# An index row between two gathers, and when the warm-up matmuls run

## The chip, the core and the metric

The kernel runs on one core of a Trainium2 chip. The time is the device time of one launch in microseconds (us); a run's time is taken without a profile, and one further execution is taken with the hardware profiler. TensorE (PE) multiplies, VectorE (DVE) and ScalarE (ACT) do elementwise work, GpSimd (POOL) makes indices and constants and issues the indirect DMAs, SyncE (SP) issues the other DMAs. Two DMA queues matter here: q1, which SP feeds, and q0, which POOL feeds. Both are served by the same 16 DMA engines.

## The reference

```python
x: (8, 3008, 256) float32
X = np.fft.fft(x, axis=1); X = np.fft.fft(X, axis=2); a = X.real      # both transforms, real part
h = np.maximum(a.reshape(24064, 256) @ w_in, 0.0)                     # w_in (256, 2048)
out = (h * h) @ w_out                                                 # w_out (2048, 256)
```

## The kernel before

The transform over the 256 features is linear, so it is multiplied into the first weight matrix: `gmat(c)` makes, for each of four blocks of 512 columns of `w_in`, the products of `w_in` with a cosine matrix (`pc`, kept as G1) and a sine matrix (`ps`, kept as G2). `gcast(c)` turns the float32 block `wst[c]` to float16 first: blocks 0 and 1 on ScalarE, 2 and 3 on VectorE. `dmats()` makes the cosine and sine matrix `csD` itself: from a row of descending numbers, `jrow`, that POOL writes (L149), four VectorE operations (L212 to L216), a fifth one later (L202), and two sines on ScalarE (L222, L223). `jrow` and its work space lie in `wst[0]`, that is, in the buffer into which the first quarter of `w_in` is loaded afterwards; so `load_w_in` (L760, four DMAs on SP) waits until L223 has read it.

The transform over the sequence uses its symmetry. A batch of 3008 rows is loaded twice: two plain loads by SP (slots 0 and 1 of `x4`) and the same rows in reversed order by indirect gathers on POOL (slots 2 and 3). For batch 0 the reversed rows come in four half gathers, `gather_half(0, s, q)` (L99), in the order slot 3 second half, slot 2 second half, slot 3 first half, slot 2 first half. VectorE adds the plain and the reversed rows (L360, L364, the "fold"), once for each half, then sums and differences (L369, L373) give `w`, the operand of the first matmuls. `stage1_first` runs these: nine matmuls on the first half (`s1[0]`), and three and six on the second half (`s1[1]`, `s1[2]`), against the tables `cosT` and `sinT`, into sums named `pf`. ScalarE copies one of each pair of sums (`as`, L484) and VectorE writes `pt` and `qt` (L493, L489).

From `pt`, `qt` and G each step (chunk c, part u) makes `xb` by TensorE, ScalarE and VectorE apply the ReLU and the square (`h`), and TensorE multiplies by `wout` into `po`, stored by SP. The first 16 `po` matmuls of a tile read the four quarters of `wout` in turn; these are loaded by four DMAs on POOL (`load_w_out`, L766), which stand behind the two gathers of batch 1 (`load_x(1)`, L112), which wait until the fold of batch 0 has read `x4` (L364).

The kernel's schedule is manual: each engine runs its instructions in the order in which the code issues them, with waits where data or buffers require them. Before the first sums, TensorE runs `warm_up(6)`: matmuls on a zeroed tile `ez`, whose result nothing reads; two more (`warm_up(2)`) stand between `s1[0]` and `gmat(0)`. They wait for POOL's memset of `ez` (L339), which stands behind the gathers and three index rows.

In the order of the code: the gathers and `jrow` (L145 to L151), tables and folds with the loads between them (L771 to L791), warm-ups and first sums (L798 to L812), and then the loop over the steps. L74 is the helper through which all matmuls go.

Of the kernel before, what the change touches and what calls it, by code (L numbers as in the profile page):

```python
# [24 lines left out]
def kernel(  # L25
# [7 lines left out]
    nc = tc.nc  # L33
    B, S, D = x.shape
    _, F = moe_w_in.shape
    P = 128
# [3 lines left out]
    QH = NQ // 2  # L40
# [32 lines left out]
    def mm(o, l, r, start, stop):  # L73
        nc.tensor.matmul(o, l, r, start=start, stop=stop, skip_group_check=True)  # L74

    def iota(name, shape, pattern, base, mult, dt=F32):
        t = const.tile(shape, dt, name=name)
        nc.gpsimd.iota(t, pattern=pattern, base=base, channel_multiplier=mult,
                       allow_small_or_imprecise_dtypes=True)
        return t  # L80
# [8 lines left out]
                   allow_small_or_imprecise_dtypes=True)  # L89
# [8 lines left out]
    def gather_half(b, s, q):  # L98
        nc.gpsimd.indirect_dma_start(  # L99
            out=x4[0:NP, 2 + s, q : q + QH, :].rearrange("p q d -> p (q d)"),  # L100
            out_offset=None,
            in_=bass.AP(tensor=x.tensor, offset=x.offset,
                        ap=[[QH * D, B * S // QH], [1, QH * D]]),
            in_offset=bass.IndirectOffsetOnAxis(ap=idx3[0:NP, 0:1], axis=0),
            element_offset=(b * S + (s + 1) * M - NQ * NP + q) * D)
# [16 lines left out]
    def load_mid(b, eng):  # L122
        for s in range(2):
            row = x[b : b + 1, s * M : s * M + 1]
            if b == 0:
                for sl, n in (((0, 1), (3, 1)), ((1, 2),))[s]:
                    eng.dma_start(out=x4[NP : NP + 1, sl : sl + n].rearrange("p s q d -> p (s q) d"),
                                  in_=row.to_broadcast([1, n * NQ, D]))
            else:
                r = s * NQ + 1  # L130
                r2 = (3 - s) * NQ + NQ - 2
                eng.dma_start(out=xm[:, r : r2 + 1 : r2 - r], in_=row.to_broadcast([1, 2, D]))
# [9 lines left out]
    for s in range(2):  # L142
        nc.sync.dma_start(out=x4[0:NP, s, :, :], in_=up(0, s))
    load_mid(0, nc.sync)
    for q in (QH, 0):  # L145
        for s in range(2):
            gather_half(0, 1 - s, q)
    jrow = jm[:, 0]
    nc.gpsimd.iota(jrow, pattern=[[-1, P]], base=P - 1, channel_multiplier=0,  # L149
                   allow_small_or_imprecise_dtypes=True)  # L150
    idx = iota("idx", [P, 1], [[0, 1]], NP - 1, -1, I32)  # L151
    idx2 = iota("idx2", [P, 1], [[0, 1]], NQ // 2 * (NP - 1), -NQ // 2, I32)
    wout16 = const.tile([P, NFC, D], F16, name="wout16")
# [161 lines left out]
    def win16(c):  # L315
        if c // 2 not in winh:
            winh[c // 2] = bfp.tile([P, 2, 1024], F16, name="win16", tag="w")
        return winh[c // 2][:, :, c % 2 * 512 : c % 2 * 512 + 512]

    def gcast(c, cp):  # L320
        cp(win16(c), wst[c])

    def gmat(c):
        cs = slice(c * 512, (c + 1) * 512)
        pc = psx.tile([P, 512], F32, name="pc", tag="x")
        for t in range(2):
            mm(pc, cosD[:, t, :], win16(c)[:, t, :], t == 0, t == 1)
        ps = psx.tile([P, 512], F32, name="ps", tag="x")
        for t in range(2):
            mm(ps, sinD[:, t, :], win16(c)[:, t, :], t == 0, t == 1)  # L330
        act(G1[:, cs], pc, AF.Copy, bias=0.0, scale=-1.0 / HS)  # L331
        act(G2[:, cs], ps, AF.Copy, bias=0.0, scale=1.0 / HS)  # L332

    def gneg(c):
        cs = slice(c * 512, (c + 1) * 512)
        ts(out=G3[:, cs], in0=G2[:, cs], scalar1=s3[:, 0:1], scalar2=None, op0=ALU.mult)
# [197 lines left out]
    for n in sizes:  # L534
        segs = []
        o = 0
        while o < n:
            b, i = divmod(g + o, NK)
# [255 lines left out]
    def warm_up(n):  # L794
        for _ in range(n):
            mm(warm, ez[:, 1, 0, :], ez[:, 1, 0:4, :], True, True)

    warm_up(6)  # L798
    gcast(0, nc.scalar.copy)
    hi_ops = []  # L800
    s1 = stage1_first(hi_ops)
    s1[0]()
    warm_up(2)
    gmat(0)
    s1[1]()
    s1[2]()
# [11 lines left out]
    side = {}  # L818
# [4 lines left out]
            side.setdefault(lo + int((hi - lo) * i / len(ops)), []).append(f)  # L823

    for c in range(1, F // 512):
        side.setdefault(c * (c - 1) // 2, []).extend([lambda c=c: gmat(c), lambda c=c: gneg(c)])

    spread(rd1[0:], 0, 5)
    spread(fo, 9, 10)
# [136 lines left out]
```

## Time and profile before

| | us |
|---|---|
| median of 4 runs (603.56 to 605.47) | 605.1 |
| the profiled execution, its own time | 602.61 |
| its span, first to last instruction | 600.7 |
| TensorE busy before 10 us / 10 to 23 / 23 to 46 / after 46 | 0.48 / 9.21 / 20.74 / 550.13 |
| VectorE busy in the same stretches | 6.41 / 8.98 / 22.67 / 485.95 |
| ScalarE busy | 7.41 / 7.84 / 22.25 / 510.81 |
| POOL busy | 8.12 / 5.25 / 0.88 / 149.97 |
| mean busy share of the DMA engines | 0.76 / 1.00 / 0.89 / 0.38 |
| memory traffic of the DMA, GB/s | 220 / 302 / 143 / 84 |

In a line of the timeline the first number is the start, the second the time from the first to the last end of a group of like instructions, then the engine, the line of the code, the operation, output and inputs, and in brackets the engine's idle time just before and what ended it. In a line of a DMA queue there stand packets, megabytes and the time of the packets as a share of 16 engines' time in the stretch.

### The profile page before, as it was taken

What the parts mean: (1) busy time and instruction counts of PE and PEld (TensorE: products, weight loads), DVE (VectorE), ACT (ScalarE), POOL (GpSimd) and SP (SyncE); (2) the same over time, 40 slices, a digit from 0 to 9 for tenths busy, and PEclk for the clock granted to TensorE, in tenths of its full rate; (3) what the DMA queues carried; (4) which work ended last, traced back from release to release, by engine and by line L of the source; (5) the groups of instructions that cost most, each with busy time, mean ns of one, the idle gap of its engine ahead of it and who ended that gap; (6) DMA issues with size and microseconds to landing.
All of it is one profiled execution on the core that took longest, in us unless ns stands there. A gap on an engine that the chain in (4) does not pass through costs nothing.

```text
span 600.7 us, 12237 instructions
## 1 busy us (share of the span) xinstructions
PE 580.6 (97%) x4543; PEld 436.4 (73%) x4543; DVE 524.0 (87%) x959; ACT 548.3 (91%) x963; POOL 164.2 (27%) x156
## 2 busy tenths in 40 slices
PE   1889999999999999999999999999999999999997
PEld 0566677777777777777877778777787778877786
DVE  6899898998898998897899997899889899999880
ACT  7799899999989999989998989999998999999981
POOL 5301023122331223213022143422543423324400
PEclk9999999999999999999999999999999999999999
DMA  8986485564583314813233115133242231332112
GB/s 225 303 98 165 103 244 174 166 224 56 69 239 45 60 55 87 222 40 49 54 59 45 53 39 68 36 47 57 57 63 42 54 49 55 51 55 56 56 53 71
DMA packets 41952, 56.24 MB, mean 94 GB/s; under 512 B 7746, under 2 KB 36726, under 8 KB 41894
## 3 DMA queue, kind: packets, MB, share of 16 engines
q1 hardware_dynamic: 37030, 42.04, 33.0%
q0 software_dynamic: 4864, 13.44, 8.8%
q8 instruction: 35, 0.57, 0.4%
q14 instruction: 23, 0.19, 0.1%
HBM read 29.02 MB, written 24.64 MB: 89 GB/s over the span
## 4 chain that ended last, share of the span: by engine, by line
PE 91%; ACT 5%; DMA 2%; DVE 1%; issue 1%; POOL 0%; ACTq 0%; DVEq 0%; POOLq 0%
PE po L74 53%; PE xb L74 31%; PE pf L74 6%; DMA x<-in_x_dram,idx 2%; ACT h L671 1%; ACT h L738 1%; ACT h L747 0%; ACT G L332 0%; ACT h L748 0%; ACT os L618 0%; ACT h L726 0%; POOL x L99 0%; ACT bs L713 0%; ACT G L331 0%; DVE bs L716 0%
## 5 line engine op out<-in xcount | busy, mean ns | idle before, releaser
L74 PE MATMUL po<-wout,h 128*128 128x256 f16 x3024 | 450.0, 272 | 0.7 <-ACT os L618 0.5
L74 PEld LDWEIGHTS <-h 128*128 128x128 f16 x3024 | 286.1, 98 | 110.4 <-issue 2.1
L74 PE MATMUL xb<-qt,G 128*128 128x512 f16 (+10 forms) x743 | 207.1, 321 | 1.6 <-ACT h L671 1.2
L714 POOL TENSOR_TENSOR bs<-bs,h 128x512 f32<-128x512 f32 x92 | 118.5, 1291 | 316.1 <-ACT bs L713 256.8
L727 DVE CUSTOM_DVE_ANT_0 h<-xb,bs 128x512 f16<-128x512 f32 (+1 forms) x231 | 145.0, 640 | 22.8 <-ACT h L726 20.6
L74 PE MATMUL xb<-pt,G 128*128 128x512 f16 (+16 forms) x512 | 146.3, 323 | 1.0 <-DVE h L727 0.4
L726 ACT ACTIVATE h<-xb 128x512 f16<-128x512 f32 (+1 forms) x218 | 135.4, 623 | 7.8 <-PE xb L74 5.5
L750 DVE TENSOR_TENSOR h<-h 128x2048 f16<-128x2048 f16 (+1 forms) x113 | 137.3, 1216 | 0.8 <-ACT h L738 0.7
L74 PEld LDWEIGHTS <-G 128*128 128x128 f16 x1255 | 120.2, 98 | 24.4 <-issue 3.4
L671 ACT ACTIVATE h<-xb 128x512 f16<-128x512 f32 (+1 forms) x166 | 104.1, 630 | 8.5 <-PE xb L74 7.6
L738 ACT ACTIVATE h<-xb 128x512 f16<-128x512 f32 (+2 forms) x155 | 96.0, 623 | 9.4 <-PE xb L74 7.8
L716 DVE SCALAR_TENSOR_TENSOR bs<-xb,h 128x512 f32<-128x512 f32 (+1 forms) x126 | 83.1, 660 | 18.7 <-PE xb L74 15.4
L748 ACT ACTIVATE h<-h 128x1024 f16<-128x1024 f16 (+1 forms) x79 | 84.8, 1074 | 0.0
L747 ACT ACTIVATE h<-h 128x1024 f16<-128x1024 f16 (+1 forms) x79 | 83.8, 1061 | 0.1
L697 DVE TENSOR_SCALAR h<-eb,gE 128x512 f16<-128x512 f16 (+1 forms) x198 | 70.3, 370 | 0.0
L618 ACT ACTIVATE os<-po 128x512 f32<-128x512 f32 (+1 forms) x95 | 59.5, 627 | 8.9 <-PE po L74 8.9
L713 ACT ACTIVATE bs<-xb 128x512 f32<-128x512 f32 x92 | 57.3, 623 | 3.2 <-PE xb L74 2.0
L112 POOL DMA_INDIRECT x<-in_x_dram,idx x16 | 21.0, 1313 | 77.0 <-DVE u L364 60.2
L360 DVE TENSOR_TENSOR u<-x 127x765 f16<-127x765 f32 x32 | 29.6, 950 | 1.3 <-DMA x<-in_x_dram,idx 1.3
L74 PEld LDWEIGHTS <-w 127*128 127x128 f16 (+1 forms) x192 | 22.2, 120 | 10.8 <-DVE w L373 4.5
L74 PE MATMUL pf<-cosT,w 127*128 127x377 f16 (+1 forms) x96 | 20.8, 329 | 3.9 <-DVE w L373 3.6
L373 DVE TENSOR_TENSOR w<-v 127x384 f16<-127x384 f16 x64 | 22.2, 371 | 0.0
(111 smaller groups left out, 213.0 us busy)
## 6 DMA issues: line engine op xcount, KB each, us to landing
out_dram<-os SPq DMA_DIRECT2D x157, 128.0 KB
x<-in_x_dram SPq DMA_DIRECT2D x16, 756.0 KB
wst<-in_moe_w_in_dram SPq DMA_DIRECT2D x4, 512.0 KB
eb<-qt SPq DMA_DIRECT2D x14, 128.0 KB
wout<-in_moe_w_out_dram POOLq DMA_DIRECT2D x4, 256.0 KB, 15.6
x<-in_x_dram,idx POOLq DMA_INDIRECT x20, 10.1
gE<-G SPq DMA_DIRECT2D x16, 0.2 KB
x<-in_x_dram SPq DMA_DIRECT2D x14, 2.0 KB
```

Source lines behind the costliest of these rows:

```text
L74: nc.tensor.matmul(o, l, r, start=start, stop=stop, skip_group_check=True)
L618: act(os_[:, js], po[:, js], AF.Copy, bias=0.0, scale=HS * HS)
L671: act(r_s(c, u), xb, AF.Relu, scale=-1.0)
L697: ts(out=X, in0=ebc[c][:, 0:n], scalar1=gE2[:, u : u + 1], scalar2=None, op0=ALU.mult)
L714: nc.gpsimd.tensor_tensor(T, T, X, op=ALU.add)
L716: stt(out=T, in0=xb, scalar=-2.0, in1=X, op0=ALU.mult, op1=ALU.add)
L726: act(r_s(c, u), xb, AF.Relu, scale=-1.0)
L727: mirrors.append((int(DEFER[c][u]), lambda: relu_d(c, u, lambda o, i: nc.vector._custom_dve(TENSOR_ADD_SAT, out=o[:, 0, :], in0=xb[:, 0, i ...
L738: relu_d(c, u, lambda o, i: act(o, xb[:, :, i], AF.Relu, scale=-1.0))
L747: act(h2[:, 0:nf], h2[:, 0:nf], AF.Square)
L748: rest.append(lambda: act(h2[:, nf:], h2[:, nf:], AF.Square))
L750: vt(h2, h2, h2, op=ALU.mult)
```

## The change

The index row `jrow` is written by POOL between the second and the third half gather instead of behind the fourth. Ten warm-up matmuls run before the first sums instead of six, and none between `s1[0]` and `gmat(0)` instead of two. The steps at which the weight blocks 1, 2 and 3 are made are written as a list instead of a formula. The words that came with the change also name the first weight cast as standing behind the first sums' copies; the diff has no line that moves a cast.

```diff
     load_mid(0, nc.sync)
-    for q in (QH, 0):
-        for s in range(2):
-            gather_half(0, 1 - s, q)
     jrow = jm[:, 0]
-    nc.gpsimd.iota(jrow, pattern=[[-1, P]], base=P - 1, channel_multiplier=0,
-                   allow_small_or_imprecise_dtypes=True)
+    for i in range(4):
+        gather_half(0, 1 - i % 2, (QH, 0)[i // 2])
+        if i == 1:
+            nc.gpsimd.iota(jrow, pattern=[[-1, P]], base=P - 1, channel_multiplier=0,
+                           allow_small_or_imprecise_dtypes=True)
...
-    warm_up(6)
+    warm_up(10)
     gcast(0, nc.scalar.copy)
     hi_ops = []
     s1 = stage1_first(hi_ops)
     s1[0]()
-    warm_up(2)
+    warm_up(0)
     gmat(0)
...
     for c in range(1, F // 512):
-        side.setdefault(c * (c - 1) // 2, []).extend([lambda c=c: gmat(c), lambda c=c: gneg(c)])
+        side.setdefault((0, 1, 3)[c - 1], []).extend([lambda c=c: gmat(c), lambda c=c: gneg(c)])
```

## The prediction

> **What bounds the kernel now.** I read the page first: TensorE is the engine that ends the chain almost everywhere.
>
> ```profile
> PE 580.6 (97%) x4543; PEld 436.4 (73%) x4543; DVE 524.0 (87%) x959; ACT 548.3 (91%) x963; POOL 164.2 (27%) x156
> PE 91%; ACT 5%; DMA 2%; DVE 1%; issue 1%; POOL 0%; ACTq 0%; DVEq 0%; POOLq 0%
> ```
>
> By a table of stages, 550.1 of the 554.7 us after 46 us are TensorE-busy, and nothing in the diff touches them. So only the first 46 us matter, and I read their timeline next.
>
> ```profile
> 7.73 0.26 POOL L149 IOTA wst<- 128x128 f32 x1
> 8.03 1.78 DVE L212 TENSOR_SCALAR wst<-wst,pidx 128x128 f32<-128x128 f32 x1 [1.70 <-POOL wst L149]
> 8.07 1.39 POOL L339 MEMSET ez<- 128x1536 f16 x1
> 9.52 2.74 PE L74 MATMUL warm<-ez 128*128 128x512 f16 x6 [9.52 <-POOL ez L339]
> ...
> 11.47 0.41 ACT L223 ACTIVATE csD<-wst,hpi 128x127 f16<-128x127 f32 x1 [0.46 <-DVE wst L202]
> 11.96 2.00 SPq L760 DMA_DIRECT2D wst<-in_moe_w_in_dram  x4
> 13.61 0.96 DVE L360 TENSOR_TENSOR u<-x 127x765 f16<-127x765 f32 x1 [1.25 <-DMA x<-in_x_dram,idx]
> 15.85 1.13 PE L74 MATMUL pf<-cosT,w 127*128 127x377 f16 x3 [3.58 <-DVE w L373]
> 18.66 1.06 PE L74 MATMUL warm<-ez 128*128 128x512 f16 x2
> 20.75 3.13 POOL L766 DMA_DIRECT2D wout<-in_moe_w_out_dram  x4
> 21.10 0.65 PE L74 MATMUL pf<-cosT,w 127*128 127x377 f16 x3
> 22.31 0.55 DVE L493 TENSOR_TENSOR pt<-as,pf 128x377 f16<-128x377 f32 x1 [2.42 <-ACT as L484]
> ```
>
> Three things are to be seen. The row `jrow` (L149) comes 1.70 us too late for VectorE. The first sums start when the second reversed gather has landed (13.6 us), not when an engine is free. And TensorE is slow until about 21 us, although the granted clock reads 1.00 throughout: the 377-column matmuls start 0.31 us apart at 15.85 and 0.16 apart at 21.1; the 512-column ones 0.43 apart.
>
> Then the DMA queues in two stretches (first 9.9 to 13.4 us, then 23 to 28):
>
> ```profile
> q0 software_dynamic: 204, 0.78, 97.3%
> ...
> q0 software_dynamic: 140, 0.73, 56.1%
> q1 hardware_dynamic: 113, 0.63, 47.1%
> ```
>
> Between 9.9 and 13.4 us the gathers (q0) alone fill the 16 engines. When both queues have work, packets alternate about one to one (140 against 113).
>
> Last, what follows. From 24 to 46 us ScalarE is busy 21.58 of 22.00 us and the chain of waits runs through it; and at 38.30 us TensorE meets the third quarter of `wout`:
>
> ```profile
> 38.30 0.60 PE L74 MATMUL po<-wout,h 128*128 128x256 f16 x4 [0.21 <-DMA wout<-in_moe_w_out_dram]
> 38.73 0.38 PE L74 MATMUL xb<-qt,G 128*128 128x256 f16 x2
> 39.22 0.71 ACT L738 ACTIVATE h<-xb 128x512 f16<-128x512 f32 x1
> ```
>
> TensorE has waited 0.21 us there for the transfer. So two things are due together at 38.3 us: ScalarE's work and a DMA.
>
> **The change, part by part.** (a) `jrow` between the gathers. It moves past two gather issues on POOL. POOL's total is the same (0.26 us), so the third and fourth gathers are issued some 0.3 us later, and the memset of `ez` and the first warm-up stay at 9.5. The delayed issues are hidden: q0 has a backlog until 15 us. `jrow` is ready at about 5.1; VectorE is free at 6.33 (end of the second L268), so L212 starts 1.7 us earlier. VectorE needs 1.40 us from the end of L212 to L202 (9.81 to 11.21 now). If L212 costs the 0.24 us of its neighbour L213, L202 comes at about 8.0; if it, like L212 now, runs into POOL's memsets, it ends near 9.8. ScalarE's L283 ends at 9.20, so L223 ends at 9.8 to 10.25 instead of 11.88: 1.6 to 2.1 us earlier. The first fold still waits for its gather (landed 11.2 by the trace's completion events), the second for 13.6: VectorE's and ScalarE's gain as such is hidden.
>
> What is not hidden: SP's L760, the load of `w_in`, waits for L223, so 2 MB of weights start 1.6 to 2.1 us earlier as well, and nothing else on SP is queued before them. Their first packet came 1.5 us after the issue (13.48), so now at 11.4 to 11.9, among the gathers. Price of that for the second gather: its slowest engine has 2.1 us left, at about 0.45 us for each 6,144-byte packet here some 5 packets, and one 2,048-byte packet of 0.10 to 0.15 us goes between each pair: +0.5 to 0.7. Bounds: 0, if that engine's share is already through; +2.1, if `w_in` took half the time. I take +0.55, nearest to the alternation shown. The fold, the first sums, and behind the fold's L364 the POOL queue (two gathers of the next batch, then four `wout` issues) all move by it.
>
> (b) Ten warm-ups for six: four more at 0.43 us, so until 13.97 instead of 12.26. They cost nothing: the first sums wait for w until 15.85. (c) The two at 18.66 go: −0.85 us at the slow clock. What both do to the clock is the open cost; no row shows what ten give. Six left the array slow, then a 3.58 us gap, and 5.1 us of unbroken matmuls (15.85 to about 20.97) made it fast. From below, the clock opens with the warm-ups and stays open over a gap of now 2.4: nine first sums take 9 x 0.16 = 1.45 instead of 2.83; pc and ps follow (4 x 0.22) at 18.7; the second half's w, now at 18.97, comes at 19.5, its nine matmuls end at 20.95, and pt (22.31 now) starts at 20.5: −1.8 us. From above, it opens as late as now: first sums from 16.4, pc and ps until 20.9, the rest half slow, until about 22.5: 0, against 22.55 now.
>
> The Trainium skill, "TensorE: Matmul & The Clock Gate", Part 1, says that the array runs at half rate until one free-running window of about 3.4 us has been busy, and goes back after an idle one. The trace's factor of two and its gap of 3.58 us fit. By the rule, ten warm-ups of 0.427 us hold a whole window of 3.41 us in about (4.27 − 3.41)/3.41 = 25% of executions, an estimate from that page: on average it would make the start 0.45 us earlier where the row's lower bound makes it 1.8, so it speaks against this part of the change; with the wait named below the sum is 602.5 us by either.
>
> (d) The steps at which the later weight blocks are made are written out as (0, 1, 3), which is what the formula gives: nothing. A first weight cast that moves behind the first sums' copies is not in the diff: the cast of block 0 stands before the sums' copies on ScalarE in both, and the orders of ScalarE, VectorE and SP, waits included, are the same. Cost 0.
>
> **The sum.** Start of ScalarE's chain: 0 to −1.8 us. But TensorE works in order, and its `po` matmuls at 35.84, 37.05 and 38.30 each need one more quarter of `wout`. The third has already been waited for. DMA runs at a share of 1.0 from 10 to 23 us and q0 alone fills it from 28.5 to 38.3, so bytes that `w_in` gains in the queue are lost by the others, and the same sum of bytes ends at the same time; with q0's issue 0.55 later, +0 to +0.55. If TensorE comes early it stands at 38.30 all the same, and L738 behind it starts at 39.1 at the earliest (38.73 + 0.38) instead of 39.22. Gain: 0.1. The part of −1.8 that came before is eaten by this wait. On the profiled execution's own 602.61 (600.7 of span and 1.9 around it) that makes 602.5. The median of the runs shown is 605.1, 2.5 above the profiled one, so the forecast on it is 605.0, with its own range of 604.2 to 605.9 (+0.45 for late `wout`, and the scatter of the runs).
>
> **Rivals.**
>
> *The early start is carried through: 603.3.* 605.1 − 1.8. For it: the profiled execution is 2.5 us faster than the median, so in the timed ones something is later that the trace doesn't show; if that is the slow clock, `wout` is there before TensorE and the whole 1.8 counts. Against: the 0.21 us of waiting, and the busy DMA. Chance 0.29.
>
> *The weights get ahead of the gathers: 606.7.* One mechanism: the early `w_in` packets hold up the second gather. Fold, first sums and, through L364, the next batch's gathers and `wout` come later by the same time. It decides once that gather lands more than about 0.6 us late, since then TensorE's first sums and `wout` are both later than now; at the middle between that and the bound of 2.1 (1.4, plus a colder array, 0.2) 605.1 + 1.6 = 606.7. For it: q0 at 97.3% between 9.9 and 13.4, with no room for a second queue. Against: packets of 2,048 bytes against 6,144. Chance 0.21.
>
> *The change doesn't do what it says: 605.1.* The clock stays slow through the warm-ups, the third part isn't there, and `jrow` comes early for a VectorE that then waits for the gather. Chance 0.10.
>
> **How the numbers follow.** Forecast 0.40, rivals 0.29, 0.21, 0.10. A measurement of this kernel tells about 0.2% (1.2 us) from no change. Of the first rival 0.26 lies beyond it, of the second 0.19; the forecast's and the last one's tails add 0.04 and 0.03. So faster 0.30, slower 0.22, same 0.48. The range that leaves out two in ten goes from 603.2 to 606.6.
>
> **What would show it.** Right: L212 at about 6.4 us; L760 near 10; the second L360 later than 13.61 by about half a microsecond; matmuls of 0.16 us from the first sum on; pt near 20.5; and TensorE waiting one to two microseconds for `wout` before 38.3, with L738 near 39.1. Wrong: a `po` matmul of the third quarter well before 38 us without a wait (first rival), or a second L360 after 14.5 us (second rival).

## The result, and the profile after

| | before | after |
|---|---|---|
| median of all runs side by side, us | 604.79 (602.28 to 606.09, 61 runs) | 603.05 (601.27 to 605.09, 40 runs) |
| ratio, 95% interval | | 0.9973 [0.9967, 0.998] |
| the profiled execution, its own time / span, us | 602.61 / 600.7 | 602.84 / 601.0 |

The changed kernel is faster by 0.27% (1.7 us). The two profiled executions don't show it: that of after is 0.2 us *longer*. Of the 61 runs of before only three lie as low as 602.61; the execution that the prediction was worked out on was an untypical one. So a second profile of the unchanged kernel was taken (the first experiment, 604.14 us, near its median), and the comparisons below are made against that one.

The page of after, the lines that answer to the two shown first:

```profile
PE 579.9 (96%) x4545; PEld 436.7 (73%) x4545; DVE 523.8 (87%) x959; ACT 548.6 (91%) x963; POOL 164.9 (27%) x156
PE 91%; DMA 4%; ACT 1%; POOL 1%; issue 1%; DVE 1%; POOLq 0%; ACTq 0%; DVEq 0%
```

DMA stands where ScalarE stood in the chain (4% against 2%, ScalarE 1% against 5%). TensorE's work is the same (4545 matmuls against 4543: ten warm-ups instead of eight). The start of the timeline of after:

```profile
4.84 0.26 POOL L149 IOTA wst<- 128x128 f32 x1
6.25 0.28 DVE L212 TENSOR_SCALAR wst<-wst,pidx 128x128 f32<-128x128 f32 x1
7.89 1.39 POOL L339 MEMSET ez<- 128x1536 f16 x1
7.93 1.69 DVE L202 TENSOR_SCALAR wst<-wst 128x128 int32<-128x128 int32 x1
...
9.34 4.02 PE L74 MATMUL warm<-ez 128*128 128x512 f16 x10 [9.34 <-POOL ez L339]
9.66 0.40 ACT L223 ACTIVATE csD<-wst,hpi 128x127 f16<-128x127 f32 x1 [0.25 <-DVE csD L221]
10.15 2.29 SPq L760 DMA_DIRECT2D wst<-in_moe_w_in_dram  x4
...
12.10 0.96 DVE L360 TENSOR_TENSOR u<-x 127x765 f16<-127x765 f32 x1 [0.91 <-DMA x<-in_x_dram,idx]
14.34 0.66 PE L74 MATMUL pf<-cosT,w 127*128 127x377 f16 x3 [0.98 <-DVE w L373]
...
19.59 0.55 DVE L493 TENSOR_TENSOR pt<-as,pf 128x377 f16<-128x377 f32 x1 [1.22 <-ACT as L484]
```

The row is early and VectorE no longer waits for it (L212 has no bracket); its last operation L202 now meets POOL's memset and takes 1.69 us; `w_in` is issued at 10.15 instead of 11.96; three first sums take 0.66 us instead of 1.13, the fast clock; and `pt` is written at 19.59. Further on in the same timeline:

```profile
35.87 0.60 PE L74 MATMUL po<-wout,h 128*128 128x256 f16 x4 [2.64 <-DMA wout<-in_moe_w_out_dram]
37.06 1.01 PE L74 MATMUL po<-wout,h 128*128 128x256 f16 x4 [0.38 <-DMA wout<-in_moe_w_out_dram]
38.72 1.06 PE L74 MATMUL po<-wout,h 128*128 128x256 f16 x4
```

TensorE waits 2.64 us for the first quarter of `wout`. The groups after it take 1.01 us instead of 0.60: in this execution the clock closed behind the wait.

### The profile page after: what moved, and what is told of

Read it like the earlier page. It is cut to its first block, busy times and chain, and to the rows that moved or that the text cites. A ratio compares the mean times of both kernels' runs of the same rounds, so it can differ in the third digit from the quotient of the medians.

```text
span 601.0 us, 12241 instructions
## 1 busy us (share of the span) xinstructions
PE 579.9 (96%) x4545; PEld 436.7 (73%) x4545; DVE 523.8 (87%) x959; ACT 548.6 (91%) x963; POOL 164.9 (27%) x156
## 4 chain that ended last, share of the span: by engine, by line
PE 91%; DMA 4%; ACT 1%; POOL 1%; issue 1%; DVE 1%; POOLq 0%; ACTq 0%; DVEq 0%
PE po L74 54%; PE xb L74 31%; PE pf L74 6%; DMA wout<-in_moe_w_out_dram 3%; DMA x<-in_x_dram,idx 1%; POOL x L99 0%; POOL x L112 0%; ACT h L747 0%; ACT os L618 0%; ACT h L726 0%; ACT bs L713 0%; DVE bs L716 0%; DVE h L727 0%; DVE h L697 0%; ACT h L748 0%
```

## The experiments

Sixteen kernels in four sets; the kernels of a set ran on one chip, with runs of the kernel before beside them (medians 604.67, 604.81, 604.86 and 605.18). A ratio is always to those. This table is read from single profiled executions: of the two profiles of the kernel before, of the changed kernel, and of the other kernels of the first set and the first two of the second. Its columns are used below: when `w_in` is issued (L760), when `pt` is written (L493), TensorE's wait for `wout` in all, the start of the fourth group of `po` matmuls (from which on all of `wout` is there), the granted clock from 34 to 42 us, and the span.

| kernel | `w_in` | `pt` | wait | fourth `po` | clock | span | median | ratio |
|---|---|---|---|---|---|---|---|---|
| before, first profile | 11.96 | 22.31 | 0.21 | 38.95 | 1.00 | 600.7 | | |
| before, again | 11.96 | 20.00 | 3.14 | 40.99 | 0.57 | 602.1 | 604.92 | 1.0006 |
| after | 10.15 | 19.59 | 3.02 | 40.00 | 0.79 | 601.0 | 603.05 | 0.9973 |
| row alone | 10.15 | 19.67 | 2.77 | 38.57 | 1.00 | 599.5 | 602.72 | 0.9974 |
| warm-ups 10 and 0 alone | 11.96 | 19.78 | 4.56 | 41.90 | 0.57 | 602.8 | 604.40 | 0.9997 |
| warm-ups 10 and 2 | 11.96 | 19.76 | 3.39 | 41.01 | 0.59 | 602.5 | 604.63 | 1.0003 |
| row, `w_in` held | 11.86 | 19.28 | 3.31 | 40.11 | 0.79 | 601.0 | 604.43 | 0.9997 |
| `w_in` early, row late | 9.32 | 21.12 | 1.69 | 38.95 | 1.00 | 599.8 | 601.79 | 0.9961 |

The span follows the fourth `po` and not `pt`: from before again to row alone the one falls by 2.42 us and the span by 2.6, from before again to after by 0.99 and 1.1, while `pt` moves by 0.3 and 0.4. This holds while TensorE waits for `wout`. In the two rows with the least waiting, the first and the last, the fourth `po` starts at the same 38.95; their spans differ by 0.9 us and their `pt` by 1.2, so there the start counts again (more on this after the fourth set).

### First set: the parts

*The kernel before, unchanged.*

> The kernel before, unchanged, for the scatter of its executions and a second profile. Theory C (the clock): the profiled execution of before was a lucky one, and a typical one, some 2 us longer, has its first fast matmul later than 21 us. Theory D (the transfers): a typical one has the second reversed gather or wout landing later than in the first profile (13.6 and 38.2 us), with the clock no different. Ratio to before 1.000 by both.

604.92 us, ratio 1.0006 [0.9993, 1.0019]. Its timeline, in the typical execution:

```profile
11.96 2.23 SPq L760 DMA_DIRECT2D wst<-in_moe_w_in_dram  x4
14.50 1.13 PE L74 MATMUL pf<-cosT,w 127*128 127x377 f16 x3 [2.24 <-DVE w L373]
20.00 0.55 DVE L493 TENSOR_TENSOR pt<-as,pf 128x377 f16<-128x377 f32 x1 [1.46 <-ACT as L484]
...
36.77 1.01 PE L74 MATMUL po<-wout,h 128*128 128x256 f16 x4 [3.14 <-DMA wout<-in_moe_w_out_dram]
38.05 1.01 PE L74 MATMUL po<-wout,h 128*128 128x256 f16 x4
```

The second gather has landed by 12.0 us, not 13.6, and the start is 2.3 us earlier than in the first profile, with nothing changed. All of it is lost again: TensorE waits 3.14 us for `wout`, and behind the wait it runs at half speed. So the late `wout`, a wait of 0.21 us in the first profile, is what ends the start-up of this kernel.

*The index row alone:* the hunk with `gather_half` and `iota` from the change; six and two warm-ups as before.

> Only the index row moved; six and two warm-ups as before. Theory C: the early fold is hidden behind the gathers, the array is as slow as before until 20 us or later: ratio 0.999 to 1.001. Theory D: most of the change's 1.7 us comes with it: ratio about 0.9975, w_in issued near 10.2 us, the second fold near 12 us.

602.72 us, 0.9974 [0.9964, 0.9985]: the whole gain of the change.

```profile
35.23 0.60 PE L74 MATMUL po<-wout,h 128*128 128x256 f16 x4 [1.93 <-DMA wout<-in_moe_w_out_dram]
36.67 0.60 PE L74 MATMUL po<-wout,h 128*128 128x256 f16 x4 [0.63 <-DMA wout<-in_moe_w_out_dram]
37.92 0.60 PE L74 MATMUL po<-wout,h 128*128 128x256 f16 x4 [0.21 <-DMA wout<-in_moe_w_out_dram]
```

In the timeline of this kernel the first quarter is there at 35.23, 1.54 us sooner than in the second profile of before, and the clock stays open (0.60 us for each group).

*The warm-ups alone.*

```diff
-    warm_up(6)
+    warm_up(10)
...
-    warm_up(2)
+    warm_up(0)
```

> Only the warm-ups: ten before the first sums, none between; the index row as before. Theory C: all of the change's gain, ratio about 0.997, first sums 0.16 us apart, the first clock event near 13 us. Theory D: at most 0.3 us, ratio 0.9995 to 1.000.

604.40 us, 0.9997 [0.9985, 1.0008]. The first sums are fast (three in 0.66 us) and `pt` comes 0.22 us earlier; the wait for `wout` is 4.56 us instead of 3.14. So the early start is eaten by that wait, as the forecast had it. Only 0.2 of the 1.42 us more are the earlier start: the first quarter of `wout`, issued at 19.40 in both executions, is there at 37.98 instead of 36.77. With ten warm-ups and the two kept it is there at 36.80, so this looks like scatter between single executions.

*Ten instead of six, the two kept.*

> Ten warm-ups before the first sums, and the two in between kept. Theory C: like the run without the two, since the two now cost 2 x 0.216 at the fast clock and TensorE waits there for the first weight cast anyway: ratio about 0.997. Theory D: 0.9995 to 1.001. If the two slow warm-ups were the point, it stays at 1.000 while the run without them gains.

604.63 us, 1.0003 [0.9992, 1.0015]: nothing.

### Second set: how the row works

*The row moved, but the load of `w_in` held.* An extra ScalarE operation, which reads the row's buffer, stands behind four operations of `mi0`, and the load behind it.

```diff
-    for f in mi0[0:0] + [dmats_fin, lambda: load_w_in(0, 1, 2, 3)] + mi0[0:] + [dmats_hi] + fe[0]:
+    hold = lambda: act(hint, jm[:, 0, 0:1], AF.Copy, bias=0.0, scale=1.0)
+    for f in [dmats_fin] + mi0[0:4] + [hold, lambda: load_w_in(0, 1, 2, 3)] + mi0[4:] + [dmats_hi] + fe[0]:
```

> The index row moved as in the change (warm-ups six and two), but the load of w_in made to wait for one more ScalarE operation, so that it is issued near 12 us as before. Theory W (the change works through the earlier load of w_in, which lets wout land earlier): the gain of 0.26% is gone, ratio 0.999 to 1.001, TensorE waits for wout until 36.5 us or later. Theory V (it works through VectorE and ScalarE, which have the tables and folds done earlier): the gain stays, ratio about 0.9975.

604.43 us, 0.9997 [0.9981, 1.0012].

```profile
11.86 2.10 SPq L760 DMA_DIRECT2D wst<-in_moe_w_in_dram  x4
...
19.28 0.55 DVE L493 TENSOR_TENSOR pt<-as,pf 128x377 f16<-128x377 f32 x1 [1.27 <-ACT G L332]
...
36.23 1.01 PE L74 MATMUL po<-wout,h 128*128 128x256 f16 x4 [3.31 <-DMA wout<-in_moe_w_out_dram]
```

VectorE and ScalarE have their early row, `pt` is the earliest of the table (19.28), and the gain is gone. (The profiled execution, 603.02, was the fastest of its twelve.)

*`w_in` early, the row late.* The row gets a work space of its own, so that `wst[0]` is free; one ScalarE write into `wst[0]` sets the moment of the load.

```diff
-    jm = wst[0].rearrange("p c f -> p (c f)")[:, 0 : 3 * P].rearrange("p (a b) -> p a b", a=3)
+    jm = const.tile([P, 3, P], F32, name="jm")
...
+    act(wst[0][:, 0, 0:1], r23, AF.Copy, bias=0.0, scale=1.0)
+    load_w_in(0, 1, 2, 3)
     dmats_fin, dmats_hi = dmats()
...
-    for f in mi0[0:0] + [dmats_fin, lambda: load_w_in(0, 1, 2, 3)] + mi0[0:] + [dmats_hi] + fe[0]:
+    for f in [dmats_fin] + mi0[0:] + [dmats_hi] + fe[0]:
```

> The index row late as before, but in a buffer of its own, so that the load of w_in doesn't wait for it and is issued near 9.5 to 10 us. Theory W: the gain is there without the row moved, ratio 0.996 to 0.998, wout's first quarter used before 36 us. Theory V: none, 0.9995 to 1.0005; slower, 1.001 or more, if the weights hold up the gathers, as one rival of the prediction had it.

601.79 us, 0.9961 [0.9945, 0.9977]: the gain without the row, and at least as much. `pt` comes 1.1 us *later* than in the second profile of before.

```profile
9.32 1.95 SPq L760 DMA_DIRECT2D wst<-in_moe_w_in_dram  x4
...
35.70 0.60 PE L74 MATMUL po<-wout,h 128*128 128x256 f16 x4 [0.94 <-DMA wout<-in_moe_w_out_dram]
```

So the row works through the load that it releases, and not through the engines that compute from it. Nor is it that `wout` is merely issued sooner: with `w_in` held it is issued at 18.87, the earliest of the table's kernels, and the first quarter is there only at 36.23; here it is issued at 20.69 and there at 35.70.

*`wout` ahead of the next batch's gathers, on the changed kernel.* `load_w_out` moves in front of `load_x(1)` on POOL. A copy of one element of `w` by POOL keeps the loads from starting at once, among batch 0's gathers.

```diff
-    for f in rd1[0:0] + fe[1][0:3] + [lambda: load_x(1)] + fe[1][3:]:
+    gate = const.tile([P, 1], F16, name="gate")
+    nc.gpsimd.tensor_copy(gate[k, :], bf[0][k, 0, 0, 0:1])
+    load_w_out()
+    for f in fe[1][0:3] + [lambda: load_x(1)] + fe[1][3:]:
         f()
-    load_w_out()
```

> The changed kernel with the four loads of wout put ahead of the two gathers of the next batch on POOL (held by a one-element copy that reads w, so not before about 14.5 us). If wout's landing is what ends the start-up, TensorE no longer waits there, the clock stays open, and it is about 3 us faster than before: ratio about 0.995 to before. If wout only happens to land where something else is due too, at most 0.5 us beyond the change: 0.9965 or more.

599.78 us, 0.9923 [0.9902, 0.9944]. With the wait gone the kernel is 5 us faster than before. (Its profiled execution, 603.82, was the slowest of its seven: its second gather landed at 13.81, and the clock fell to half from 16.88 to 23.71.)

*The kernel before, with 14 matmuls in the wait.* They multiply G1 by itself into the first `po` bank, just before its first real matmul, and nothing reads their result.

```diff
+                    if c == 0 and grp is groups[0]:
+                        for _ in range(14):
+                            mm(st["o"].rearrange("p a b -> p (a b)"), G1[:, 0:P], G1[:, 0:512], True, True)
```

> The kernel before, with 14 matmuls of 512 columns into the first po bank just ahead of its first real matmul (3.0 us at the fast clock, in the wait for wout). If the clock's closing after that wait costs time of its own, the clock events show none between 21 and 595 us and the run is some 1 to 1.5 us faster than before: 0.9975 to 0.9985. If ScalarE's work covers the slow matmuls, 1.000; slower where wout is early and the matmuls are in the way.

603.83 us, 0.9983 [0.9967, 0.9998]. In every execution the mean granted clock is 0.997 to 1.0 (before again: 0.991 to 0.997). Keeping the clock open over the wait is worth about 1 us (604.81 − 603.83; 0.1 to 2.0 by the interval), though the matmuls themselves are work added.

### Third set: what is left without the wait

The same move of `wout` on the kernel before, on the kernel with the row alone, on the changed kernel once more, and there together with the early `w_in`.

> The kernel before, with the loads of wout put ahead of the next batch's gathers as in the run of the changed kernel; row, load of w_in and warm-ups as before. If the wait for wout and the clock's closing behind it were all that the change removed, this alone is as fast as the changed kernel with the same edit (0.9923): 0.992 to 0.993. If the start of the chain counts once wout is out of the way, it stays behind by the row's 0.3 us and the warm-ups' 0.2 to 1.3 us: 0.993 to 0.995.

> The index row moved and wout first, with six and two warm-ups. Against the changed kernel with wout first it prices the warm-ups where no wait eats them. If the prediction's working of the clock holds (up to 1.8 us between an open and a closed clock at the first sums), it is 0.5 to 1.5 us slower than that kernel: 0.9935 to 0.995. If the clock opens in time with six as well, the same: 0.992 to 0.993.

> The changed kernel with wout first, once more beside the others (the first measurement had 7 executions): 0.991 to 0.994 again, and a profile without the clock's closing at 16.9 us that the first had.

> The changed kernel with wout first and the load of w_in near 9.5 us (the index row in a buffer of its own). If the first weight cast, which waits for w_in, is what ends the first sums' stage, a further 0.3 to 0.6 us: 0.991 to 0.992. If the early weights now hold up the gathers, slower than the run beside it by 0.5 us or more.

601.41 us (0.994 [0.9921, 0.9959]); 599.93 (0.9919 [0.9894, 0.9943]); 599.78 (0.9923 [0.9898, 0.9948]); 599.78 (0.9921 [0.9896, 0.9946]). The timeline of the third:

```profile
14.85 3.15 POOL L766 DMA_DIRECT2D wout<-in_moe_w_out_dram  x4
...
18.30 1.07 POOL L112 DMA_INDIRECT x<-in_x_dram,idx  x1 [0.30 <-DVE w L373]
...
33.74 0.60 PE L74 MATMUL po<-wout,h 128*128 128x256 f16 x4
```

`wout` is issued at 14.85 instead of 19.24, the gathers behind it, and no `po` matmul waits. The warm-ups bring nothing here either (second against third kernel), nor does a still earlier `w_in` (third against fourth). But the row seemed to be worth 1.5 us still (601.41 against 599.93), although nobody waits for `wout` any more, and the intervals overlap. If that were real, the row would work by a second way.

### Fourth set: is there a second way

The pair once more, and between its two the kernels that have the row without the early load, and the early load without the row.

> Row moved, w_out loads ahead of the next batch's gathers, w_in held back to about 11.9 us. Theory 1 (the row works only through the moment at which w_out lands; with w_out loaded first TensorE doesn't wait for it, so nothing is left for the row): 599.8 to 600.6, equal within 0.7 us to the other three of this batch. Theory 2 (the early w_in helps also where nobody waits for w_out): slow, near 601.4. Theory 3 (with w_out first the row works through VectorE and ScalarE themselves): fast, near 599.9.

> Row late as before, w_out loads first, w_in issued near 9.3 us by a work space of its own for the row. Theory 1: equal within 0.7 us to the other three. Theory 2: fast, near 599.9. Theory 3: slow, near 601.4.

> The kernel before with w_out loaded first, once more. It had 601.41. Theory 1: that was chance, it comes to 600.0 to 600.8. Theories 2 and 3: 601.2 to 601.6, 1.5 us above the kernel with the row moved.

> Row moved and w_out loaded first, once more; it had 599.93. All theories: 599.7 to 600.2. Its distance to d3 is what the row brings when nobody waits for w_out: below 0.7 us by theory 1, 1.3 to 1.7 us by theories 2 and 3.

600.45 us (0.9938 [0.9917, 0.996]); 600.54 (0.9939 [0.9918, 0.996]); 600.64 (0.9931 [0.991, 0.9952]); 601.69 (0.9944 [0.9925, 0.9964]). The row unmoved is now 1.05 us *ahead* of the row moved, so the expectation for the last one (599.7 to 600.2) was missed by 1.5 us: from the third set to the fourth the one kernel went down by 0.8 us and the other up by 1.8. Over both sets the medians are 601.0 without the row (15 runs) and 600.7 with it (13). Where nobody waits for `wout`, no gain of the row can be told from none; the first theory stands, within about 1 us.

The profiles show where this scatter arises. In the eight of these two sets, the span less the start of `pt` is 578.2 to 578.6 us, while `pt` itself starts anywhere from 19.72 to 21.57. The first profile of before, with its wait of 0.21 us, fits in (600.7 − 22.31 = 578.4), and so nearly does `w_in` early (578.7). With a wait for `wout` it is more: 582.1 in the second profile of before, 581.7 with `w_in` held, 581.4 after, 579.8 with the row alone. So where TensorE doesn't wait, a later or earlier start is carried through to the end in full; what lies above 578.4 is the price of a late `wout`, 3.7 us in the second profile of before and 1.4 with the row alone. What the row could win without a wait it would win through `pt`: 20.36 and 19.92 with it, 20.52 and 20.92 without, one execution each, too few to tell.

## Why the prediction was right or wrong

**The wait that was to eat the early start was there, and it did.** The warm-ups opened the clock and made the first sums fast, as (b) and (c) held possible, but `pt` won only 0.2 us by it in a like execution and the time nothing. That the warm-ups (four more, two fewer) are worth nothing came out as forecast; the list (d) gives the same numbers as the formula.

**The step that failed is in the sum: "bytes that `w_in` gains in the queue are lost by the others, and the same sum of bytes ends at the same time".** It took a busy share of 1.0 for a fixed rate. Here is the DMA view of 14 to 18 us, first of the second profile of before, then of the row alone (queue; packets, megabytes, time of the packets as a share of 16 engines):

```profile
DMA packets 501, 0.97 MB, mean 244 GB/s; under 512 B 25, under 2 KB 25, under 8 KB 501
q1 hardware_dynamic: 501, 0.97, 97.0%
```

```profile
DMA packets 782, 1.50 MB, mean 376 GB/s; under 512 B 48, under 2 KB 48, under 8 KB 782
q1 hardware_dynamic: 782, 1.50, 100.4%
```

The engines are busy in both, all of it with q1, and move 0.97 or 1.50 MB in the same 4 us. Most packets of 2,048 bytes take 84 ns (the median), but with the late load about 5% of them take 300 to 500 ns until about 17.5 us. In the kernels of the table with `w_in` at 10.15 or earlier the stretch moved 358 to 376 GB/s; with `w_in` at 11.86 or later, 230 to 275. Three executions with a late second gather (13.5 us or after) lie between, 298 to 318: the first profile of before, the kernel with 14 matmuls in the wait, and, although its `w_in` was early, the first one with `wout` ahead. A late gather alone doesn't decide it: `w_in` early, row late, reads its second gather at 13.55 and moves 358. By 18 us that is 5.00 MB against 4.23 from the span's start. Why the late packets are slow is open: that the load's moment decides is shown, its cause isn't. So bytes were not exchanged but gained, and what stands behind them in the queues ended earlier: the third quarter of `wout`, which the forecast held at 38.3, was used at 39.71 in the second profile of before, at 38.72 after and at 37.92 with the row alone. The forecast's gain of 0.1 became 1.7.

**The clock behind the wait was a second term that the sum didn't have.** A table of stages from 34 to 42 us (columns: stretch, length, busy time and count of TensorE, its weight loads, VectorE, ScalarE and POOL, granted clock, DMA share, GB/s), of the second profile of before, of after, and of the row alone:

```profile
34.00:42.00 8.00, 5.23 (x28) 3.75 (x28) 5.95 (x18) 6.51 (x14) 0.00 (x0) 0.57 0.99 106
```

```profile
34.00:42.00 8.00, 5.75 (x38) 4.47 (x38) 5.81 (x18) 6.98 (x16) 0.00 (x0) 0.79 0.68 73
```

```profile
34.00:42.00 8.00, 5.93 (x48) 4.63 (x48) 7.23 (x19) 7.76 (x17) 0.00 (x0) 1.00 0.54 54
```

TensorE begins 28, 38 and 48 matmuls in the same time, for 5.23, 5.75 and 5.93 us of being busy. A shorter wait for `wout` wins twice: by itself, and by the clock that stays open. Of the executions of after, those with a mean clock of 0.994 have a median of 603.26 us (16), those with 0.996 one of 602.87 (10), those with 0.997 one of 602.48 (16).

**What was taken from the first profile alone was off.** The first sums at 15.85, `pt` at 22.31 and the wait of 0.21 us belong to an execution whose second gather landed 1.6 us late. In it the start really was late enough to meet `wout`, which hid the largest term. The prediction had seen that the profiled execution was 2.5 us below the median, and carried that difference through unexplained in the forecast, as a slow clock in the first rival; by the second profile the right reading was a wait for `wout` of 3 us.

**The rivals.** The early start carried through (603.3) gave nearly the measured time by the wrong way: `wout` was not there before TensorE, and a kernel with an early start and a late load (`pt` at 19.28) gains nothing. The near hit of that rival's number is luck. The weights getting ahead of the gathers delayed nothing in a like pair of executions: the second gather landed at 11.98 with the row alone and at 12.04 in the second profile of before. Whether (a)'s +0.55 us, from `w_in` packets that alternate with the gathers', exists is open: over all 18 profiles that gather landed at 11.47 to 13.81 where `w_in` was issued by 10.16 (nine, median 12.38) and at 11.38 to 13.59 where it was issued later (nine, median 11.72), a scatter wider than the term. The change does what it says, apart from the part that isn't in the diff.

**The other numbers of (a)** held: L212 at 6.25 (about 6.4 was said) for 0.28 us, L202 caught by POOL's memset and over at 9.62 (9.8), L223 over at 10.06 (9.8 to 10.25), `w_in` at 10.15. Only the first packet of `w_in` came later than said, at 12.06 instead of 11.4 to 11.9. `pt` came at 19.59, not 20.5, for the reason above.

**The rule** weighed against (b), from the Trainium skill, "TensorE: Matmul & The Clock Gate", Part 1, gave ten warm-ups a full window in an estimated 25% of executions. In all six profiles with ten the clock was open by the third of the first sums (three in 0.65 to 0.85 us); with six it was so in two of twelve. The measurement decides: ten do more than the rule's estimate gave them, though in one of the six the clock fell again at 16.88. It made no difference to the time that these runs can tell.

**A better version.** The changed kernel with `wout` loaded first took 599.78 us twice, 0.9923 [0.9902, 0.9944] and 0.9923 [0.9898, 0.9948], below the interval of the change itself; without the row and the warm-ups the same move gives 0.994 and 0.9931, with the row and without the warm-ups 0.9919 and 0.9944, so what the change adds to it isn't shown.

## What to carry to other kernels

Take a second profile of the kernel before working out a sum of a few tenths of a per cent, when the profiled execution lies at the edge of the runs: a wait of 0.21 us in one execution was 3.14 in the typical one. A load that is released by a small computation has its place in the queue by that computation; test the load's moment by itself (hold it, then free it) before crediting the engines. And where a weight load stands in a queue behind gathers that wait for a buffer, let it pass them: here that was worth two to three times the change (3.4 and 4.5 us on the kernel before, against 1.7).

## What the runs showed of the hardware that was not expected

- A DMA share of 0.97 to 1.00 went with 244 and with 376 GB/s, with the same 2,048-byte packets.
- After a wait of TensorE the granted clock fell to half for about one stretch of 3.4 us (2.64 us of wait, after: (1 − 0.79) x 8 / 0.5 = 3.4) or two (3.14 us, before again: (1 − 0.57) x 8 / 0.5 = 6.9), and not at all after 1.93 us (row alone). The wait's length does not settle it: 3.31 us, with `w_in` held, cost one stretch. It fell after another wait too: in the first kernel with `wout` ahead TensorE waited 2.37 us for `w`, until 16.07, and the clock was 0.50 from 16.88 to 23.71 (two stretches).
- A VectorE operation on 128 x 128 elements takes 0.22 to 0.28 us alone and 1.69 to 1.78 beside POOL's memset of 1.39 us: L212 before the change, L202 after it. The change moved the collision, it didn't end it.
